# Attention with the keys on the partitions: the exps are used as they come, V is stationary, the mask is added by a matmul

## The chip, the cores and the metric

One core of one Trainium2 chip runs the kernel. The metric is the time of one execution on the device in microseconds (us); the median of the runs stands for the kernel. The engines named below are PE (matmuls and transposes), DVE and ACT (elementwise work; ACT also has the exponential), POOL (constants, selections, and issuing some transfers) and SP, which here only issues transfers. Each works through its own queue in order. Matmul results land in PSUM, eight banks of 512 f32 per partition, and are copied from there to SBUF.

## The reference

Block-sparse attention on 4 batch entries, 8 heads, 768 tokens and a head dimension of 64, and then a mixture of 8 experts of which each token takes one. Everything is f32.

```
scores = q @ k.T / sqrt(64)
mask   = neighbouring 32-blocks, first and last block, 3 sampled blocks per row of blocks
attn   = exp(where(mask, scores, -1e9) - rowmax);  attn /= attn.sum(-1) + 1e-9
x      = (attn @ v), heads side by side            # 3072 tokens x 512
logits = x @ w_gate;  e = argmax;  g = softmax(logits)[e]
out    = g * (relu(x @ w1[e]) @ w2[e])             # w1: 512 x 1024, w2: 1024 x 512
```

The inputs q, k and v are normal numbers times 0.1, so that the scores lie near zero.

## The kernel before, in words

The kernel has three stages. The attention works on 16 pairs of heads (4 batch entries, 4 pairs each). A pair has 6 chunks of 128 tokens; chunk c holds the tokens 6p + c, p being the partition, so that a transfer reads long runs. `load` (L79) fetches k, q and v of a pair through SP, one pair ahead. `turn` (L147) transposes k and q on PE (L155) so that the head dimension lies on the partitions: head 0 on partitions 0 to 63, head 1 on 64 to 127.

A unit is one chunk of 128 queries of a pair; there are 96. `scores` (L165) multiplies the queries as stationary operand with all 768 keys (L173), two matmuls per head. A head has 64 rows of the array, and the two heads' matmuls alternate. One DVE instruction (L181) adds the mask, which lies in SBUF as 0 or -2^33 per query and key, and takes the row's extreme; ACT forms the exps and their sum (L186). Queries are on the partitions at that point, and the next matmul has to contract over keys. So `turn_e` (L190) transposes the 12 blocks of exps on PE (L197) and copies them back in three parts (L199 on DVE, L201 on ACT). `attend` (L205) makes each transposed block stationary and moves the 64 columns of V past it (L209), 12 matmuls per unit, divides by the sums (L213 to L215) and writes 128 columns of x. `route` (L220) transposes the finished x once more (L225, L227) and adds the pair's part of the logits (L230, L235); `keep_x` stores x to DRAM, `gate` the gate weights at a batch entry's end.

The mask is built once at the start: which blocks attend to which (`allow`, with the sampled blocks from DRAM), which query lies in which block (`rows`), their product on PE (L136) and its widening to 768 keys on DVE (L141, L142). The 16 MB of w1 are fetched to SBUF by POOL (L94).

The second stage, the routing (L297 to L411), sorts the tokens by expert: POOL makes constants, DVE computes slots, PE sums (L349, L350, L404). The third stage takes 31 tiles of 128 tokens: POOL gathers their rows of x (L424), SP fetches w2 of the tile's expert (L432), PE runs both layers (L447, L469), POOL scatters the results (L472).

The order of the work is written out in the loop at L268: scores of unit u, transposes of unit u - 1, attend of unit u - 2, route of unit u - 4. A planner then simulates the engines by a cost model and may move an instruction ahead of others on its engine when its operands and buffers come free earlier; it also sets all semaphores. The profile's order on PE thus differs a little from the code's. A buffer that is named with bufs=2 exists twice, and a third use waits until the first is released.

Of the kernel before, what the change touches and what calls it, by code (L numbers as in the profile page):

```python
# [8 lines left out]
F32 = mybir.dt.float32  # L9
# [9 lines left out]
def kernel(  # L19
# [11 lines left out]
    nc = tc.nc  # L31
# [5 lines left out]
    NCH = S // P  # chunks of 128 tokens; chunk c holds the tokens NCH * p + c  # L37
    CW = NCH // 2 * P  # columns of half the chunks, within one PSUM bank
# [31 lines left out]
    ps_t = att.enter_context(tc.tile_pool(name="ps_t", bufs=2, space=PSUM))  # L70
    ps_o = att.enter_context(tc.tile_pool(name="ps_o", bufs=2, space=PSUM))
    ld = att.enter_context(tc.tile_pool(name="ld", bufs=2))
    work = att.enter_context(tc.tile_pool(name="work", bufs=2))
    small = att.enter_context(tc.tile_pool(name="small", bufs=4))
    xpool = att.enter_context(tc.tile_pool(name="xpool", bufs=2))

    loaded, turned = {}, {}

    def load(b, pr):  # L79
        got = []  # L80
        for src, nm in ((k, "k_sb"), (q, "q_sb")):
            t = ld.tile([P, NCH, 2, D], F32, name=nm)
            for hh in range(2):
                nc.sync.dma_start(t[:, :, hh, :], src[b, 2 * pr + hh].rearrange("(p c) d -> p c d", p=P))  # L84
            got.append(t)
        t = ld.tile([P, 2, NCH, D], F32, name="v_sb")
# [6 lines left out]
    def load_w1(e):  # L93
# [4 lines left out]
    mask = mpool.tile([P, NCH, S], BF16, name="mask")  # L98

    def make_mask(pool):  # L100
        # Which blocks of keys (columns) a block of queries (partitions) attends to.
# [24 lines left out]
        # rows[n, t, p]: whether query NCH * p + t lies in block n.  # L126
        rows = pool.tile([NB, NCH, P], F32, name="rows")
        nc.vector.memset(rows[:], 1.0)
        for base, cm, st, sp in ((0, -BLK, 1, NCH), (BLK - 1, BLK, -1, -NCH)):
            nc.gpsimd.affine_select(  # L130
                out=rows[:], in_=rows[:], compare_op=ALU.is_ge, fill=0.0, base=base, channel_multiplier=cm,
                pattern=[[st, NCH], [sp, P]],
            )
        bm = ps_o.tile([P, NCH, NB], F32, name="bm", tag="o")
        for t in range(NCH):
            nc.tensor.matmul(bm[:, t, :], lhsT=rows[:, t, :], rhs=allow[:], start=True, stop=True)  # L136
        pen = pool.tile([P, NCH, NB], F32, name="pen")
        nc.vector.tensor_scalar(pen[:], bm[:], scalar1=-MASKED, scalar2=MASKED, op0=ALU.mult, op1=ALU.add)
        for t in range(NCH):
            wide = pool.tile([P, NB, BLK], BF16, name="wide", bufs=2)  # L140
            nc.vector.tensor_copy(wide[:], pen[:, t, :].unsqueeze(2).to_broadcast([P, NB, BLK]))  # L141
            nc.vector.tensor_copy(  # L142
                mask[:, t, :].rearrange("p (c j) -> p c j", c=NCH),
                wide.rearrange("p n o -> p (n o)").rearrange("p (j c) -> p c j", c=NCH),
            )

    def turn(b, pr):  # L147
        k_sb, q_sb, v_sb = loaded.pop((b, pr))
        outs = []
        for src, nm in ((k_sb, "kT"), (q_sb, "qT")):  # L150
            dst = work.tile([P, S], F32, name=nm)
            for half in range(2):
                tp = ps_t.tile([P, CW], F32, name="tp", tag="t")
                for c in range(NCH // 2):
                    nc.tensor.transpose(  # L155
                        tp[:, c * P : (c + 1) * P], src[:, half * (NCH // 2) + c].rearrange("p h d -> p (h d)"), ident[:],
                    )
                if half == 0:
                    nc.vector.tensor_copy(dst[:, :CW], tp[:])
                else:  # L160
                    nc.scalar.copy(dst[:, CW:], tp[:])
            outs.append(dst)
        turned[(b, pr)] = (*outs, v_sb)

    def scores(b, pr, t):  # L165
        kT, qT, v_sb = turned[(b, pr)]
        ss = small.tile([P, 2], F32, name="ss")
        es = []
        sps = [ps_s.tile([P, 2, 512], F32, name="s") for hh in range(2)]
        for j in range(2):  # L170
            for hh in range(2):
                r = slice(hh * D, (hh + 1) * D)
                nc.tensor.matmul(  # L173
                    sps[hh][:, j, :CW], lhsT=qT[r, t * P : (t + 1) * P], rhs=kT[r, j * CW : (j + 1) * CW],
                    start=True, stop=True,
                )
        for hh in range(2):
            # The scores with their sign turned, and the least of each row: minus its maximum.
            e = work.tile([P, S], F32, name="e", bufs=4)
            nmax = small.tile([P, 1], F32, name="nmax")  # L180
            nc.vector.tensor_tensor_reduce(  # L181
                out=e.rearrange("p (j c) -> p j c", j=2), in0=sps[hh][:, :, :CW],
                in1=mask[:, t, :].rearrange("p (j c) -> p j c", j=2),
                scale=-scale, scalar=3.0e38, op0=ALU.add, op1=ALU.min, accum_out=nmax[:],
            )
            nc.scalar.activation(e[:], e[:], AF.Exp, bias=nmax[:], scale=-1.0, accum_out=ss[:, hh : hh + 1])  # L186
            es.append(e)
        return es, ss, v_sb

    def turn_e(es, ss, v_sb):  # L190
        eT = []
        for g in range(3):
            part = late.tile([P, 4, P], F32, name="eT", bufs=6)
            tp = ps_t.tile([P, 4, P], F32, name="tpe", tag="t")
            for m in range(4):
                hh, c = divmod(4 * g + m, NCH)
                nc.tensor.transpose(tp[:, m, :], es[hh][:, c * P : (c + 1) * P], ident[:])  # L197
            if g == 0:
                nc.vector.tensor_copy(part[:], tp[:])  # L199
            else:  # L200
                nc.scalar.copy(part[:], tp[:])  # L201
            eT += [part[:, m, :] for m in range(4)]
        return eT, ss, v_sb

    def attend(t, eT, ss, v_sb, xb):  # L205
        op = ps_o.tile([P, 2, D], F32, name="op", tag="o")
        for hh in range(2):
            for c in range(NCH):
                nc.tensor.matmul(  # L209
# [316 lines left out]
```

## Time and profile before

| | us |
|---|---|
| runs (3) | 1201.95, 1203.21, 1203.82 |
| median | 1203.21 |
| the profiled execution: span from first to last instruction | 1203.9 |
| of it PE busy, DVE busy, ACT busy, POOL busy | 1131.7, 414.1, 355.5, 73.8 |
| attention, to PE's last matmul of it | about 668 |
| routing, until the experts' first gathered rows land | about 668 to 699 |
| experts | about 699 to 1204 |

The profile has no time of its own beside the span; the span is what the sums below are made against, and it lies 0.7 us above the median of the runs. A matmul on f32 appears in the trace as two weight loads (PEld) and two MATMUL records, one for each pass; a transpose appears as one of each. The duration of a MATMUL record includes the time in the array's pipeline, so that successive records overlap: what a record costs is the distance between starts. "128*64" in a matmul's row is rows times columns of the array that it uses.

### The profile page before, as it was taken

Reading aid. Unit: us, or ns where it says so; the run is one execution under the profiler, and the core shown is the slowest. Engines: PE = TensorE matmul, PEld = TensorE weight load, DVE = VectorE, ACT = ScalarE, POOL = GpSimd, SP = SyncE. Lnnn points to the kernel's source line nnn. Section 1 sums busy time; section 2 is a strip of 40 time slices with the busy share of each in tenths; the row PEclk is TensorE's granted clock in tenths of the full one; section 3 lists DMA queues with packets and bytes.
Section 4 is the critical chain, followed back from the end, with each engine's and each line's share of the span. In section 5 each row is a group of like instructions: output and inputs, shape, how many; then the busy total and the mean of one; then the engine's idle time right before and its main releaser. Section 6 shows DMA issues by size and latency. Waiting matters only on the chain.

```text
span 1203.9 us, 15693 instructions
## 1 busy us (share of the span) xinstructions
PE 1131.7 (94%) x6132; PEld 756.1 (63%) x6132; DVE 414.1 (34%) x1032; ACT 355.5 (30%) x707; POOL 73.8 (6%) x101
## 2 busy tenths in 40 slices
PE   2899999999999999999999579999999999999996
PEld 1687878787877788788878534444444444444443
DVE  1654545554454444454444411111111111111110
ACT  0454545454545455455545000000000000000000
POOL 3000000000000000000000011111110111111100
PEclk9999999999999999999999679999999999999998
DMA  9911221112021212120000415544444555544441
GB/s 337 343 37 27 54 53 28 40 43 53 27 52 30 53 27 54 27 54 27 27 1 14 154 36 174 168 141 160 149 156 164 175 172 175 174 162 149 161 140 55
DMA packets 112269, 122.64 MB, mean 102 GB/s; under 512 B 56451, under 2 KB 72835, under 8 KB 112196
## 3 DMA queue, kind: packets, MB, share of 16 engines
q1 hardware_dynamic: 102484, 90.28, 24.9%
q0 software_dynamic: 9184, 31.33, 6.7%
q8 instruction: 50, 0.82, 0.3%
q14 instruction: 23, 0.19, 0.1%
q10 hardware_dynamic: 528, 0.02, 0.0%
HBM read 108.93 MB, written 14.52 MB: 103 GB/s over the span
## 4 chain that ended last, share of the span: by engine, by line
PE 54%; issue 38%; POOL 3%; DVE 2%; DMA 1%; SPq 0%; POOLq 0%; ACT 0%; DVEq 0%
PE op L209 21%; PE s L173 16%; PE tpe L197 12%; POOL xg L424 3%; PE lg L230 2%; PE tp L155 2%; DMA samp_i<-in_sampled_blocks_dram 1%; POOL out_dram L472 1%; PE tpx L225 1%; PE tok_ps L404 1%; DVE mask L142 0%; DVE wide L141 0%; PE bm L136 0%; SPq L84 0%; DVE oh_r L399 0%
## 5 line engine op out<-in xcount | busy, mean ns | idle before, releaser
L209 PE MATMUL op<-v_sb,eT 128*128 128x64 f32 x2304 | 278.5, 271 | 0.0
L209 PEld LDWEIGHTS op<-v_sb,eT 128*128 128x128 f32 x2304 | 272.4, 192 | 0.0
L186 ACT ACTIVATE e<-e,nmax 128x768 f32<-128x768 f32 x192 | 179.7, 936 | 243.6 <-DVE nmax L181 238.8
L447 PE MATMUL hp<-w_all,xgT 128*128 x496 | 223.2, 604 | 16.4 <-DVE xgT L439 16.4
L469 PE MATMUL zp<-w,hT 128*128 128x512 f32 x496 | 218.2, 593 | 1.1 <-DVE hT L462 1.1
L181 DVE CUSTOM_DVE_ANT_0 e<-s,mask 128x768 f32<-128x768 f32 x192 | 176.3, 954 | 103.2 <-PE s L173 103.2
L173 PE MATMUL s<-kT,qT 64*128 64x384 f32 x768 | 198.3, 525 | 7.8 <-DVE nmax L181 7.8
L447 PEld LDWEIGHTS hp<-w_all,xgT 128*128 128x128 f32 x496 | 92.7, 192 | 129.2 <-issue 105.9
L197 PEld LDWEIGHTS tpe<-ident,e 128*128 128x128 f32 x1152 | 127.5, 145 | 61.1 <-issue 26.7
L197 PE MATMUL tpe<-ident,e 128*128 128x128 f32 x1152 | 164.5, 279 | 0.0
L469 PEld LDWEIGHTS zp<-w,hT 128*128 128x128 f32 x496 | 91.8, 190 | 105.3 <-issue 103.8
L464 ACT COPY hT<-tph 128x512 f32<-128x512 f32 x31 | 18.2, 586 | 436.7 <-PE tph L460 436.7
L201 ACT COPY eT<-tpe 128x512 f32<-128x512 f32 x192 | 110.8, 577 | 51.0 <-PE tpe L197 50.5
L173 PEld LDWEIGHTS s<-kT,qT 64*128 64x128 f32 x768 | 79.2, 188 | 45.1 <-issue 19.6
L471 DVE TENSOR_SCALAR zo<-zp,xg 128x512 f32<-128x512 f32 x31 | 23.3, 750 | 204.3 <-PE zp L469 204.3
L452 DVE TENSOR_SCALAR h<-hp 128x512 f32<-128x512 f32 x31 | 21.4, 691 | 209.0 <-PE hp L447 209.0
L199 DVE COPY eT<-tpe 128x512 f32<-128x512 f32 x96 | 65.9, 687 | 15.5 <-PE tpe L197 15.3
L472 POOL DMA_INDIRECT out_dram<-zo,s_idx x31 | 31.6, 1018 | 431.3 <-DVE zo L471 431.3
L213 DVE TENSOR_SCALAR r<-ss 128x2 f32<-128x2 f32 x96 | 16.1, 167 | 88.1 <-ACT e L186 88.1
L215 DVE TENSOR_TENSOR xb<-op,r 128x128 f32<-128x128 f32 x96 | 28.0, 292 | 43.9 <-PE op L209 42.8
L308 POOL IOTA first_w_i<- 128x8 int32 x1 | 0.1, 135 | 657.4 <-PE op L209 657.4
L460 PEld LDWEIGHTS tph<-ident,h 128*128 128x128 f32 x248 | 30.0, 141 | 16.4 <-issue 16.4
(103 smaller groups left out, 484.0 us busy)
## 6 DMA issues: line engine op xcount, KB each, us to landing
w<-in_moe_w_dram SPq DMA_DIRECT2D x31, 2048.0 KB, 10.4
w_all<-in_moe_w_dram POOLq DMA_DIRECT2D x8, 2048.0 KB, 27.3
k_sb<-in_k_dram SPq DMA_DIRECT2D x32, 192.0 KB, 3.4
q_sb<-in_q_dram SPq DMA_DIRECT2D x32, 192.0 KB, 3.3
v_sb<-in_v_dram SPq DMA_DIRECT2D x16, 384.0 KB, 3.4
x_rows<-xb SPq DMA_DIRECT2D x16, 384.0 KB, 4.3
xg<-x_rows,g_idx POOLq DMA_INDIRECT x31, 7.8
out_dram<-zo,s_idx POOLq DMA_INDIRECT x31, 8.0
```

Source lines behind the costliest of these rows:

```text
L173: nc.tensor.matmul(sps[hh][:, j, :CW], lhsT=qT[r, t * P : (t + 1) * P], rhs=kT[r, j * CW : (j + 1) * CW], start=True, stop=True,)
L181: nc.vector.tensor_tensor_reduce(out=e.rearrange("p (j c) -> p j c", j=2), in0=sps[hh][:, :, :CW], in1=mask[:, t, :].rearrange("p (j c) -> ...
L186: nc.scalar.activation(e[:], e[:], AF.Exp, bias=nmax[:], scale=-1.0, accum_out=ss[:, hh : hh + 1])
L197: nc.tensor.transpose(tp[:, m, :], es[hh][:, c * P : (c + 1) * P], ident[:])
L199: nc.vector.tensor_copy(part[:], tp[:])
L201: nc.scalar.copy(part[:], tp[:])
L209: nc.tensor.matmul(op[:, hh, :], lhsT=eT[hh * NCH + c], rhs=v_sb[:, hh, c, :], start=(c == 0), stop=(c == NCH - 1),)
L424: nc.gpsimd.indirect_dma_start(out=xg[:], out_offset=None, in_=x_d[:, :], in_offset=bass.IndirectOffsetOnAxis(ap=g_idx[:, i : i + 1], axis=0),
L447: nc.tensor.matmul(hp[:, f, :], lhsT=st[i]["xT"][:, c, :], rhs=w1_all[:, c, bass.ds(e, 1), f * 512 : (f + 1) * 512].rearrange("p e f -> p ...
L460: nc.tensor.transpose(tp[:, m, :], st[i]["h"][:, (4 * g + m) * P : (4 * g + m + 1) * P], ident[:])
L469: nc.tensor.matmul(zp[:], lhsT=st[i]["hT"][:, fb, :], rhs=st[i]["w2"][:, fb, :], start=(fb == 0), stop=(fb == FB - 1))
L472: ins = nc.gpsimd.indirect_dma_start(out=out[:, :], out_offset=bass.IndirectOffsetOnAxis(ap=s_idx[:, i : i + 1], axis=0), in_=zo[:], in_of ...
```

## The change

The stationary operand of the scores is now a chunk of 128 keys, the moving one half of the pair's queries (384), so that the scores come out with keys on the partitions and the exps can be contracted over keys without a transpose. The mask is added in PSUM by a second matmul in bf16: `oh` says which block a key lies in, `pen` holds 0 or -2^33 per block and query, twice, on partitions 0 to 63 and 64 to 127. No maximum is subtracted; ACT reads PSUM and takes exp of the scaled scores of both heads at once. DVE adds up the six exps of a half. V (128 keys x 64) is stationary in `attend`; head 0's result goes to partitions 0 to 63 of the output bank and head 1's to 64 to 127, which makes them use the left and the right half of the array's columns. The output is then transposed, and multiplied with the gate's weights, by one matmul per 128 queries with the moving operand `mix` (identity, and w_gate for each head); the sums of the exps are brought onto the query partitions by matmuls with a column of ones. The division is done afterwards, on x and on the logits' parts.

The order is by groups of two chunks of keys: scores of group i, attend of group i - 1; in the middle group of each half also half of the next pair's turn (k in the first half, q in the second) and the output of the half before. Score buffers are two of two banks each, transposes have one bank, outputs of attend two, output turns one. v has three buffers, and the second pair is loaded ahead of the loop.

At the end of the attention a check compares all sums with 2^-4 and 2^40 and all logits with -2^100 and 2^100, counts the entries that pass, and loads the verdict into registers of all engines; under `tc.If` stands a general path that does the attention again with a maximum subtracted. The mask's construction is changed accordingly. Routing and experts are as before. The core of the diff:

```diff
+    ps_t = att.enter_context(tc.tile_pool(name="ps_t", bufs=1, space=PSUM))
+    ps_x = att.enter_context(tc.tile_pool(name="ps_x", bufs=1, space=PSUM))
...
+        nc.vector.tensor_copy(oh[:], rows[:])
+        for half in range(2):
+            bm = ps_o.tile([P, HC, P], F32, name="bm", tag="o")
+            nc.tensor.matmul(bm[:], lhsT=allow2[:], rhs=rows[:NB, half * HC : (half + 1) * HC, :], start=True, stop=True)
+            nc.vector.tensor_scalar(
+                pen[:, half * CW : (half + 1) * CW].rearrange("p (t q) -> p t q", t=HC), bm[:],
+                scalar1=-MASKED, scalar2=MASKED, op0=ALU.mult, op1=ALU.add,
+            )
...
+    def scores(n, half, c):
+        b, pr = pairs[n]
+        kT, qT = turned[(b, pr)][0], turned[(b, pr)][1]
+        cols = slice(half * CW, (half + 1) * CW)
+        s = ps_s.tile([P, 2, 512], F32, name="s")
+        for hh in range(2):
+            r = slice(hh * D, (hh + 1) * D)
+            nc.tensor.matmul(s[:, hh, :CW], lhsT=kT[r, c * P : (c + 1) * P], rhs=qT[r, cols], start=True, stop=False)
+        for hh in range(2):
+            r = slice(hh * D, (hh + 1) * D)
+            nc.tensor.matmul(s[:, hh, :CW], lhsT=oh[r, c, :], rhs=pen[r, cols], start=False, stop=True)
+        e = work.tile([P, 2, CW], F32, name="e", bufs=6)
+        nc.scalar.activation(e[:], s[:, :, :CW], AF.Exp, scale=scale)
+        es[(n, half, c)] = e
+        if c == 1:
+            esums[(n, half)] = work.tile([P, 2, CW], F32, name="esum")
+        if c > 0:
+            t = esums[(n, half)]
+            nc.vector.tensor_add(t[:], es[(n, half, 0)][:] if c == 1 else t[:], e[:])
+
+    def attend(n, half, c):
+        v_sb = loaded[pairs[n]][2]
+        if c == 0:
+            ops_[(n, half)] = ps_o.tile([P, CW], F32, name="op", tag="o")
+        op = ops_[(n, half)]
+        e = es[(n, half, c)]
+        for hh in range(2):
+            nc.tensor.matmul(
+                op[hh * D : (hh + 1) * D, :], lhsT=v_sb[:, hh, c, :], rhs=e[:, hh, :], start=(c == 0), stop=(c == NCH - 1),
+            )
+        if c == NCH - 1:
+            oT = work.tile([P, CW], F32, name="oT")
+            nc.scalar.copy(oT[:], op[:])
+            ops_[(n, half)] = oT
+
+    def rows_out(n, half):
...
+        for m in range(HC):
+            for hh in range(2):
+                nc.tensor.matmul(
+                    xr[:, HC * M + 2 * m + hh : HC * M + 2 * m + hh + 1], lhsT=esum[:, hh, m * P : (m + 1) * P], rhs=ones[:],
+                    start=True, stop=True,
+                )
+        for m in range(HC):
+            nc.tensor.matmul(xr[:, m * M : (m + 1) * M], lhsT=oT[:, m * P : (m + 1) * P], rhs=mix[:, pr, :], start=True, stop=True)
...
+    GR = 2
+    steps = [(n, half, g) for n in range(len(pairs)) for half in range(2) for g in range(NCH // GR)]
+    load(*pairs[1])
+    for i in range(len(steps) + 2):
+        if i < len(steps):
+            n, half, g = steps[i]
+            if half == 1 and g == 0 and n + 2 < len(pairs):
+                load(*pairs[n + 2])
+            if half == 0 and g == 2 and n % 2 == 0 and n // 2 < E:
+                load_w(n // 2)
+            for c in range(g * GR, (g + 1) * GR):
+                scores(n, half, c)
+        if 0 <= i - 1 < len(steps):
+            n, half, g = steps[i - 1]
+            for c in range(g * GR, (g + 1) * GR):
+                attend(n, half, c)
+        if i < len(steps) and steps[i][2] == 1:
+            n, half, _ = steps[i]
+            turning = turn(*pairs[n + 1], half) if n + 1 < len(pairs) else iter(())
+            next(turning, None)
+            if i > 3:
+                rows_out(*steps[i - 2][:2])
+            for _ in turning:
+                pass
+    rows_out(*steps[-1][:2])
...
+    nc.vector.tensor_single_scalar(ok[:, :n_sums], flat, 2.0**-4, op=ALU.is_ge)
+    nc.vector.scalar_tensor_tensor(
+        ok[:, :n_sums], in0=flat, scalar=2.0**40, in1=ok[:, :n_sums], op0=ALU.is_le, op1=ALU.mult,
+    )
...
+    nc.vector.reduce_sum(okn[:], ok[:], axis=AX)
+    okp = ps_x.tile([1, 1], F32, name="okp", tag="xr")
+    nc.tensor.matmul(okp[:], lhsT=okn[:], rhs=ones[:], start=True, stop=True)
+    bad = mpool.tile([1, 1], I32, name="bad")
+    nc.vector.tensor_scalar(bad[:], okp[:], scalar1=float(P * (n_sums + n_lgn)), scalar2=None, op0=ALU.not_equal)
...
+    again = nc.values_load(bad[0:1, 0:1], min_val=0, max_val=1)
+    with tc.If(again > 0):
+        for n in range(len(pairs)):
...
```

## Rows read from the trace of the kernel before

**Rows 1.** The page's first part: busy us, share of the span, instructions of each engine
```profile
PE 1131.7 (94%) x6132; PEld 756.1 (63%) x6132; DVE 414.1 (34%) x1032; ACT 355.5 (30%) x707; POOL 73.8 (6%) x101
```

**Rows 2.** Stretches: us; PE, PEld, DVE, ACT, POOL busy (instructions); granted clock, DMA
```profile
134.00:641.00 507.00, 507.00 (x3763) 408.75 (x3761) 248.90 (x683) 256.80 (x516) 0.00 (x0) 1.00 0.15 38
...
668.00:683.00 15.00, 2.29 (x12) 1.95 (x12) 11.47 (x36) 0.72 (x2) 2.24 (x16) 0.64 0.34 97
```

**Rows 3.** The page's chain that ended last, share of the span by engine
```profile
PE 54%; issue 38%; POOL 3%; DVE 2%; DMA 1%; SPq 0%; POOLq 0%; ACT 0%; DVEq 0%
```

**Rows 4.** Stretch of one pair of heads, between two loads
```profile
254.00:293.60 39.60, 39.60 (x295) 31.87 (x295) 19.16 (x53) 19.89 (x41) 0.00 (x0) 1.00 0.16 41
```

**Rows 5.** Groups by line of that pair: xcount | busy us, mean ns | idle before
```profile
L209 PE MATMUL op<-v_sb,eT 128*128 128x64 f32 x145 | 17.7, 271 | 0.0
...
L173 PE MATMUL s<-kT,qT 64*128 64x384 f32 x48 | 12.3, 517 | 0.0
...
L197 PE MATMUL tpe<-ident,e 128*128 128x128 f32 x72 | 10.2, 278 | 0.0
```

**Rows 6.** Timeline of one unit: start us, us, engine, line, operation, xcount [idle before]
```profile
304.72 1.56 PE L173 MATMUL s<-kT,qT 64*128 64x384 f32 x8
...
306.21 0.86 PEld L197 LDWEIGHTS tpe<-ident,e 128*128 128x128 f32 x8 [0.55 <-issue]
...
307.03 2.09 PEld L209 LDWEIGHTS op<-v_sb,eT 128*128 128x128 f32 x18
```

**Rows 7.** Timeline of PE in ever later windows of the same unit's scores
```profile
305.15 1.14 PE L173 MATMUL s<-kT,qT 64*128 64x384 f32 x6
...
305.47 0.81 PE L173 MATMUL s<-kT,qT 64*128 64x384 f32 x4
...
305.79 0.49 PE L173 MATMUL s<-kT,qT 64*128 64x384 f32 x2
```

**Rows 8.** Groups by line over the whole span
```profile
L186 ACT ACTIVATE e<-e,nmax 128x768 f32<-128x768 f32 x192 | 179.7, 936 | 243.6 <-DVE nmax L181 238.8 <-DVE gw L254 4.8
...
L227 ACT COPY xT<-tpx 128x384 f32<-128x384 f32 x32 | 15.3, 479 | 15.1 <-PE tpx L225 15.1
...
L399 DVE TENSOR_TENSOR oh_r<-iota_r,rc 128x768 f32<-128x768 f32 x4 | 3.6, 953 | 0.0
```

**Rows 9.** Lines L94 and, in the window at 21.5 us, L84: issues and landings
```profile
L94 POOL DMA_DIRECT2D w_all<-in_moe_w_dram x8: 740/750/941, 2.8 to 9.7; - x8
...
DMA to landing us min/median/max: 11.8/27.3/45.7
...
L84 SPq DMA_DIRECT2D q_sb<-in_q_dram x1: 8193/8193/8193, 21.5 to 21.5; - x1
...
DMA to landing us min/median/max: 31.8/31.8/31.8
```

**Rows 10.** Timeline at the attention's end
```profile
667.84 0.29 DVE L215 TENSOR_TENSOR xb<-op,r 128x128 f32<-128x128 f32 x1 [2.55 <-PE op L209]
...
670.68 0.36 DVE L334 TENSOR_TENSOR sc<-lgn,lmax 128x192 f32<-128x192 f32 x1
...
676.81 0.16 DVE L370 CAST xe<-xe_f 1x31 int32<-1x31 f32 x1
...
678.27 1.65 SPq L432 DMA_DIRECT2D w<-in_moe_w_dram  x2
```

**Rows 11.** The page's transfers: xcount, KB each, us to landing
```profile
x_rows<-xb SPq DMA_DIRECT2D x16, 384.0 KB, 4.3
...
wg<-in_moe_w_gate_dram ACTq DMA_DIRECT2D x1, 16.0 KB, 1.9
```

**Rows 12.** Stretch 683 to 693 us; timeline of L447's first weight loads
```profile
683.00:693.00 10.00, 10.00 (x48) 10.00 (x48) 0.94 (x2) 0.00 (x0) 0.00 (x0) 0.50 0.85 317
...
702.16 0.34 PEld L447 LDWEIGHTS hp<-w_all,xgT 128*128 128x128 f32 x1 [0.52 <-issue]
703.01 0.34 PEld L447 LDWEIGHTS hp<-w_all,xgT 128*128 128x128 f32 x1 [0.52 <-issue]
```

More of the change, by code (lines that the diff above doesn't have):

```diff
@@ L85, in load @@
             got.append(t)
-        t = ld.tile([P, 2, NCH, D], F32, name="v_sb")
+        t = ld.tile([P, 2, NCH, D], F32, name="v_sb", bufs=3)
         nc.sync.dma_start(
@@ L137, in make_mask @@
[L137 to L170, printed above, removed]
+        allow2 = pool.tile([NB, P], F32, name="allow2")
+        nc.vector.memset(allow2[:], 0.0)
+        nc.vector.tensor_copy(allow2[:, :NB], allow[:])
+        nc.vector.tensor_copy(allow2[:, D : D + NB], allow[:])
+        rows = pool.tile([P, NCH, P], F32, name="rows")
@@ new lines, with turn @@
+    small = att.enter_context(tc.tile_pool(name="small", bufs=4))
+    xpool = att.enter_context(tc.tile_pool(name="xpool", bufs=2))
+    def turn(b, pr, which):
+        src = loaded[(b, pr)][which]
+        dst = work.tile([P, S], F32, name="qT" if which else "kT")
+        turned.setdefault((b, pr), {})[which] = dst
+        for half in range(2):
+            tp = ps_t.tile([P, CW], F32, name="tp", tag="t")
+            for c in range(HC):
+                nc.tensor.transpose(
+                    tp[:, c * P : (c + 1) * P], src[:, half * HC + c].rearrange("p h d -> p (h d)"), ident[:],
+                )
+            if half == 0:
+                nc.vector.tensor_copy(dst[:, :CW], tp[:])
+            else:
+                nc.scalar.copy(dst[:, CW:], tp[:])
+            yield
@@ L188, in scores @@
[L188 to L209, printed above, removed]
-                    op[:, hh, :], lhsT=eT[hh * NCH + c], rhs=v_sb[:, hh, c, :], start=(c == 0), stop=(c == NCH - 1),
-                )
-        r = small.tile([P, 2], F32, name="r")
-        nc.vector.tensor_scalar_add(r[:], ss[:], 1e-9)
-        nc.vector.reciprocal(r[:], r[:])
+        for m in range(HC):
+            nc.tensor.matmul(xr[:, m * M : (m + 1) * M], lhsT=oT[:, m * P : (m + 1) * P], rhs=mix[:, pr, :], start=True, stop=True)
@@ L215, in attend @@
+        lg = small.tile([P, HC, 2, E], F32, name="lg")
         nc.vector.tensor_tensor(
[L216 to L231 removed]
+            lg[:], got[:, :, P:].rearrange("p m (h e) -> p m h e", h=2), r[:].unsqueeze(3).to_broadcast([P, HC, 2, E]), op=ALU.mult,
+        )
@@ L241, in gate @@
+        if half == 1:
+            rows = x_d[b * S : (b + 1) * S, pr * P : (pr + 1) * P]
+            nc.sync.dma_start(rows.rearrange("(p c) w -> p c w", p=P), xb[:])
+            if pr == NPR - 1:
+                gate(b)
     def gate(b):
@@ new lines @@
+    for which in range(2):
+        for _ in turn(0, 0, which):
+            pass
[22 more added lines that the diff above has]
+            for _ in turning:
+                pass
@@ L295 @@
+    again = nc.values_load(bad[0:1, 0:1], min_val=0, max_val=1)
+    with tc.If(again > 0):
+        for n in range(len(pairs)):
+            load(*pairs[n])
+            for which in range(2):
+                for _ in turn(*pairs[n], which):
+                    pass
+            for half in range(2):
+                shifted(n, half)
+                for c in range(NCH):
+                    attend(n, half, c)
+                rows_out(n, half)
     att.close()
```

159 lines of the change are left out of this document (83 added, 76 removed).

## The prediction

> **What bounds the kernel now.** I read the page's busy times first, then the stretches, then the chain, then one pair of heads record by record. PE is busy 94% of the span, DVE 34%, ACT 30% [rows 1]. The stretches divide the span: from 134 to 641 us, inside the attention, PE is busy for every microsecond at a granted clock of 1.00; the routing behind it has PE at work for 2.3 of 15 us and a clock that falls [rows 2]. The change touches the attention and the seam behind it, so the attention's PE time is what counts. The chain agrees: PE has 54% of it, and no other engine over 3% [rows 3]; its 38% "issue" is the time before matmuls of the experts for which nothing is waited, and these stay as they are.
>
> One pair of heads takes 39.6 us, PE without a gap, DVE and ACT at half load [rows 4]. By line it is the 144 records of L209 (one matmul on f32 shows as two records, one per pass), the 48 of L173, the 72 transposes of L197 and small change [rows 5].
>
> How PE spends a record is seen in one unit [rows 6, 7]. The scores use 64 rows of the array per head, and the two heads start together: of eight records from 304.72 six are left at 305.15, four at 305.47, two at 305.79. The spacing is 0.322 us, so one f32 pass of 384 columns costs 0.839 ns a column, and two heads cost what one does. The 18 L209 weight loads of 2.09 us come every 0.112 us or so, though a record moves only 64 columns (0.054 us by the same 0.839 ns): attend is bound by loading its weights. The transposes keep much the same pace (8 from 306.21 to 307.03); I count 0.11.
>
> **The change, part by part.** I call 128 keys by 384 queries of both heads a step: 12 per pair, 192 in all.
> Removed per pair: the 72 transposes of exps (72 x 0.11 = 7.9 us of PE), their copies on DVE and ACT, 144 attend records (144 x 0.112 = 16.1 us), the mask and maximum on DVE, six route transposes.
> Scores of a step: the same kind of matmul, keys and queries exchanged: two passes of 0.322 us, heads side by side, 0.645 us.
> Mask of a step: two bf16 matmuls of 384 columns on 64 rows each, side by side as the scores are. The trace has no bf16 matmul. Above, one pass at the f32 pace, 0.32 us; below, one weight load, 0.11 us. I take 0.20, near the middle, as one short pass of narrow operands. The Trainium skill, "TensorE: Matmul & The Clock Gate", section "Back-to-back issue gap", gives columns / 2.4 + 2.5 ns for a warm bf16 matmul, an estimate of 162 ns here, by which the forecast would be 981 us; no run here shows it yet.
> Attend of a step: V stationary, 64 columns, one half of the array's columns per head, 384 columns moving in two passes. If the halves run side by side as the row halves do, 0.645 us; one after the other, 1.29 us. I take 0.645: the row halves are the nearest thing the trace shows [rows 7]. The Trainium skill, "TensorE: Matmul & The Clock Gate", section "Measured speedup vs the span model", has three column tiles at 2.38 times the pace of one, 79% of the full gain; an estimate by it is 0.81 us a step and 1018 us in all. No row of this trace has a column tile.
> Change of array shape: steps come in groups of two, scores then attend, so two changes a group. The eight score records hold PE for 1.49 us where four spacings are 1.29, 0.20 too much; the weight loads behind them idle 0.55 us [rows 6]. Between 0.20 and 0.55 I take 0.35 a group.
> A group is 2 x (0.645 + 0.20 + 0.645) + 0.35 = 3.33 us; three make 9.99 us for half a pair's queries.
> Added per half, the output's turn: six sums (12 records with a one-column operand, bound by weight loads as L209's, 12 x 0.112 = 1.34 us) and three matmuls of 144 columns (6 x 0.121 = 0.73 us): 2.06 us. Six transposes of the next pair's k or q: 0.65 us, and 0.2 us for the shape. Half: 12.9 us; pair: 25.8 us.
>
> What hides the rest. ACT per half: six exps of 768 columns, 0.94 us each as now, and two copies of 384 columns, 0.48 us each: 6.6 us. DVE per half: five adds of 768 columns at 0.953 us (L399 is that size), a copy of 384, and eight small operations, at most 0.3 us each, behind the turn: 7.7 us at most [rows 8]. Both lie under 12.9 us. Two score buffers of two banks suffice: a buffer is free one exp, some 1.1 us, after its mask, and PE comes back to it after one attend group, 1.3 us, and another step. The single transpose buffer makes the second three transposes wait for DVE; the output's turn stands between. If that cover went, it would cost PE a DVE add and a copy, some 1.5 us a half, 45 us in 30 halves.
>
> The start. Eight loads of w1 leave POOL by 9.7 us and the last lands 45.7 us later, at 55.4; behind them the second load of the second pair's q, issued at 21.5, lands after 31.8 us, at 53.3 [rows 9]. It is issued so early already that moving the second pair's loads ahead of the loop brings nothing, and w1 goes through POOL's queue as before. So even if pair 0 were started by 25 us and took 25.8, it would be done before pair 1 can begin, and part of its gain is lost. Pair 1 starts after six transposes of q and two copies (0.7 and 2 x 0.5 us) with a wait or two between, at 55.5.
> PE is through at 55.5 + 15 x 25.8 = 442.5 us.
>
> The seam. Today 2.8 us pass from the last xb to the router's first operation at 670.7 [rows 10]. The check adds five DVE operations (about 2.0 us at the 0.36 us of L334's 192 columns), a matmul and a compare (1.2, an estimate from four steps of about 0.3) and a load of the verdict into every engine's registers (1.3: xe is done at 676.97, the transfer that needs it issues at 678.27 [rows 10]): 4.5 us, with the 2.8 7.3 us. Then every engine branches over the general path. POOL's constants, 2.2 us that lay beside the attention's end [rows 2], start behind it; the router needs them one after the other, so they cost little. Nothing in the trace shows such a branch; below zero is excluded, since it only adds a wait. I allow a landing of a row write (4.3 us) and of a short load (1.9 us) [rows 11]: 6.2; the top is 16. Routing starts at 442.5 + 13.5 = 456.0.
> From there to the end 1203.9 - 670.7 = 533.2 us are unchanged: routing runs at clock 0.50 already [rows 12], so a longer idle stretch ahead takes nothing more. 456.0 + 533.2 = 989.2. The profiled execution spans 1203.9, the median of the runs is 1203.2: 988.5 us.
>
> **The rivals.**
> Columns one after the other. V's halves may not overlap: they read two different streams over all 128 partitions, where the row halves read 64 each [rows 7]. Against it: the halves of the array are as separate. Price 0.645 us x 180 steps = 116 us: 1104 us.
> The clock falls: slower than before. While the 48 small matmuls of L404 kept PE busy for 10 of 10 us, the clock stayed at 0.50, the lower of its levels of 1.2 and 2.4 GHz, and passes of 512 columns then started 0.85 us apart where 0.839 ns a column gives 0.43 [rows 12]. If half-filled arrays did that throughout, a pair would take 51.6 us: 55.5 + 774 + 13.5 + 533.2 = 1376 us. It outweighs the gain of 215 us once more than 8 of the 15 pairs run so (215 / 25.8). Against it: the row-halved scores run at 1.00 from 134 to 641 us [rows 2].
> The change doesn't do what it says: the verdict is wrong and the general path runs as well. Per half at least six blocks of 1.29 + 0.4 + 0.65 us, attend 3.9 and the turns 2.7, 21 us; 32 of them, 660 us: 1650 us or more. Against it: the sums count some hundred exps near one, far inside their limits, and the counts stay whole numbers.
>
> **How the numbers follow.** Forecast, columns side by side: 0.74, own range 950 to 1040. Its low end: mask 0.11 (-16), shape change 0.20 (-14), branch free (-6). Its high end: mask 0.32 (+22), change 0.55 (+18), branch 16 (+10). Columns in turn 0.18, around 1104. A cover gone or a finer alternation by the planner, 1040 to 1075: 0.04. Clock 0.03, general path 0.01. The range 950 to 1110 takes in the second case. Faster by over 0.2% (about what a measurement can tell from no change) 0.955, slower 0.04, the same 0.005.
>
> **What would show it.** Right: attend's records (128 rows by 64 columns) start in twos, the twos 0.32 us apart; pairs follow every 25 to 27 us with PE busy throughout at clock 1.00; DVE and ACT near half; routing begins near 456 us; the last 533 us as before. Wrong: attend records one by one 0.32 us apart (pairs of 33.5 us); a clock of 0.50 in the attention; mask records near 0.32 us; PE idle before scores with ACT or DVE as releaser, which would mean that the cover failed; a seam over 25 us.

## The result and the profile after

The changed kernel takes 969.39 us (median of 4 runs, 968.87 to 969.55) where the kernel before takes 1202.58 (1200.7 to 1203.82) beside it: a ratio of 0.8057, 95% interval 0.8046 to 0.8069. The forecast was 988.5, its range 950 to 1110. The profiled execution spans 967.7 us, which stands to the 989.2 of the prediction's sum.

The page's busy times of the changed kernel; the line answers to [rows 1].

```profile
PE 901.3 (93%) x4110; PEld 458.7 (47%) x4110; DVE 321.4 (33%) x621; ACT 221.5 (23%) x323; POOL 76.4 (8%) x103
```

A third of PE's records are gone (6132 to 4110) and more than half of ACT's (707 to 323); PE's busy time falls by 230.4 us, and the span by 236.2. No other engine has come near its limit.

Stretches of the changed kernel: us; PE, PEld, DVE, ACT and POOL busy (instructions); granted clock, DMA share, GB/s. They answer to [rows 2, 4].

```profile
60.00:400.00 340.00, 340.00 (x2260) 181.60 (x2260) 182.70 (x363) 156.37 (x218) 0.00 (x0) 1.00 0.25 61
200.00:225.30 25.30, 25.30 (x171) 13.49 (x171) 13.43 (x26) 11.64 (x16) 0.00 (x0) 1.00 0.26 63
426.00:435.00 9.00, 0.19 (x2) 0.11 (x2) 3.69 (x20) 0.24 (x1) 0.07 (x1) 0.58 0.22 54
```

PE is busy in every microsecond from 60 to 400 us, inside the attention, and at clock 1.00, as before. The second line is one pair of heads, the length that the turn's records repeat at: 25.30 us where [rows 4] have 39.6, with DVE at 13.4 and ACT at 11.6. The third is the seam: 9 us in which PE works for 0.19.

One group of two steps in the changed kernel's timeline (start us, us, engine, line, operation, xcount [idle before]); it answers to [rows 6].

```profile
208.47 0.92 PE L195 MATMUL s<-qT,kT 64*128 64x384 f32 x4
209.22 0.33 PE L198 MATMUL s<-pen,oh 64*128 64x384 bf16 x2
209.39 0.81 PE L195 MATMUL s<-qT,kT 64*128 64x384 f32 x4
209.59 1.68 ACT L200 ACTIVATE e<-s 128x768 f32<-128x768 f32 x2 [1.64 <-PE s L198]
210.03 0.33 PE L198 MATMUL s<-pen,oh 64*128 64x384 bf16 x2
210.29 1.51 PE L215 MATMUL op<-e,v_sb 128*64 128x384 f32 x8
211.73 0.59 PE L195 MATMUL s<-qT,kT 64*128 64x384 f32 x2
```

Read the starts. The second step's scores take from 209.39 to 210.03, 0.64 us; a mask from 209.22 to 209.39, 0.17; the eight attend records from 210.29 to 211.73, 1.44 us. The group takes 211.73 - 208.47 = 3.26 us. Three of them with the turn make a half of 12.65.

The same eight attend records in ever later windows, read as [rows 7] were.

```profile
210.66 1.14 PE L215 MATMUL op<-e,v_sb 128*64 128x384 f32 x6
210.99 0.81 PE L215 MATMUL op<-e,v_sb 128*64 128x384 f32 x4
211.31 0.49 PE L215 MATMUL op<-e,v_sb 128*64 128x384 f32 x2
```

Eight are left at 210.29, six at 210.66, four at 210.99, two at 211.31: they start in twos, 0.32 us apart. The two column halves run side by side.

### The profile page after: what moved, and what is told of

Read it like the earlier page. It is cut to its first block, busy times and chain, and to the rows that moved or that the text cites. A ratio compares the mean times of both kernels' runs of the same rounds, so it can differ in the third digit from the quotient of the medians.

```text
span 967.7 us, 10826 instructions
## 1 busy us (share of the span) xinstructions
PE 901.3 (93%) x4110; PEld 458.7 (47%) x4110; DVE 321.4 (33%) x621; ACT 221.5 (23%) x323; POOL 76.4 (8%) x103
## 4 chain that ended last, share of the span: by engine, by line
issue 47%; POOL 5%; PE 1%; DVE 1%; POOLq 0%; DVEq 0%
POOL xg L512 3%; POOL out_dram L560 1%; PE tok_ps L492 1%; DVE oh_r L487 0%; POOLq L609 0%; DVE oh_c L479 0%; DVE oh_c L483 0%; POOLq L512 0%; DVE sl L467 0%; POOLq L560 0%; DVE pr__10054 L432 0%; PE cps L437 0%; PE cps L438 0%; POOL lt_strict L409 0%; DVE xk L452 0%
## 5 line engine op out<-in xcount | busy, mean ns | idle before, releaser
L200 ACT ACTIVATE e<-s 128x768 f32<-128x768 f32 x192 | 155.3, 811 | 94.8 <-PE s L198 93.1
L195 PE MATMUL s<-qT,kT 64*128 64x384 f32 x768 | 167.4, 514 | 0.0
L206 DVE TENSOR_TENSOR esum<-esum,e 128x768 f32<-128x768 f32 x128 | 122.6, 958 | 71.5 <-ACT e L200 64.5
L215 PE MATMUL op<-e,v_sb 128*64 128x384 f32 x768 | 144.8, 499 | 0.0
L195 PEld LDWEIGHTS s<-qT,kT 64*128 64x128 f32 x768 | 64.1, 188 | 64.8 <-ACT e L200 38.0
L215 PEld LDWEIGHTS op<-e,v_sb 128*64 128x64 f32 x768 | 46.6, 136 | 80.1 <-issue 79.9
L198 PE MATMUL s<-pen,oh 64*128 64x384 bf16 x384 | 63.8, 326 | 0.0
L231 PEld LDWEIGHTS xr<-ones,esum 128*128 128x128 f32 x384 | 45.4, 192 | 1.8 <-DVE esum L206 1.2
L231 PE MATMUL xr<-ones,esum 128*128 128x1 f32 x384 | 45.0, 244 | 0.0
L548 PE MATMUL tph<-ident,h 128*128 128x128 f32 x248 | 36.9, 273 | 0.0
```

The source lines that it names most:

```text
L195: nc.tensor.matmul(s[:, hh, :CW], lhsT=kT[r, c * P : (c + 1) * P], rhs=qT[r, cols], start=True, stop=False)
L198: nc.tensor.matmul(s[:, hh, :CW], lhsT=oh[r, c, :], rhs=pen[r, cols], start=False, stop=True)
L200: nc.scalar.activation(e[:], s[:, :, :CW], AF.Exp, scale=scale)
L206: nc.vector.tensor_add(t[:], es[(n, half, 0)][:] if c == 1 else t[:], e[:])
L215: nc.tensor.matmul(op[hh * D : (hh + 1) * D, :], lhsT=v_sb[:, hh, c, :], rhs=e[:, hh, :], start=(c == 0), stop=(c == NCH - 1),)
L231: nc.tensor.matmul(xr[:, HC * M + 2 * m + hh : HC * M + 2 * m + hh + 1], lhsT=esum[:, hh, m * P : (m + 1) * P], rhs=ones[:], start=True, s ...
```

## The experiments

Theory: PE sets the pace throughout the attention. Steps cost 1.45 us of PE (0.645, 0.16 and 0.645), two changes of array shape 0.36 a group, the turn 2.9 a half; the heads run side by side in rows (scores) and in columns (attend); DVE and ACT are covered; the start gained by the order of loads, the seam lost to the check. Rivals: the column halves are worth nothing and something else is faster than thought; ACT or the two score buffers pace the groups; the start's gain comes from the attention's new form. Ratios are to the kernel before beside each run.

**Both heads in one column half** (the results are summed, so attend's output is another; the copy behind it is changed to match: ACT copies 64 partitions out of PSUM, and DVE copies them to the other 64).

```diff
-                op[hh * D : (hh + 1) * D, :], lhsT=v_sb[:, hh, c, :], rhs=e[:, hh, :], start=(c == 0), stop=(c == NCH - 1),
+                op[:D, :], lhsT=v_sb[:, hh, c, :], rhs=e[:, hh, :], start=(c == 0 and hh == 0), stop=(c == NCH - 1 and hh == 1),
```

> Both heads' attend matmuls go to the left half of the array's columns and are summed in one output (so x is not the reference's: the heads are mixed); all else as in the changed kernel at 969.4 us. Theory (the column halves run side by side, and PE sets the pace): the pairs of records come apart, each step's attend takes 4 x 0.322 = 1.29 us instead of 0.645, so 192 x 0.645 = +124 us, about 1093 us, and a pair of heads takes 33.0 us instead of 25.3. Rival (the starts in twos are how the records are drawn, the array works on the halves in turn anyway): no change, 969 us. Second rival (ACT's exps set the pace): under +60 us.

Measured 1093.56 us, ratio 0.9093 [0.9076, 0.9109]. Its timeline, the whole run of records and its last two windows:

```profile
205.49 2.79 PE L215 MATMUL op<-e,v_sb 128*64 128x384 f32 x8
207.47 0.81 PE L215 MATMUL op<-e,v_sb 128*64 128x384 f32 x2
207.80 0.49 PE L215 MATMUL op<-e,v_sb 128*64 128x384 f32 x1
208.21 0.55 PE L176 MATMUL tp<-ident,q_sb 128*128 128x128 f32 x3
```

Now they start one by one, 0.33 us apart, and eight take 208.21 - 205.49 = 2.72 us in place of 1.44. The 124 us are 192 steps of 0.645: what the prediction called columns side by side is shown, and without it over half of the 233 us of gain would be gone.

**No mask matmuls** (the mask is left out of the scores).

```diff
-            nc.tensor.matmul(s[:, hh, :CW], lhsT=kT[r, c * P : (c + 1) * P], rhs=qT[r, cols], start=True, stop=False)
-        for hh in range(2):
-            r = slice(hh * D, (hh + 1) * D)
-            nc.tensor.matmul(s[:, hh, :CW], lhsT=oh[r, c, :], rhs=pen[r, cols], start=False, stop=True)
+            nc.tensor.matmul(s[:, hh, :CW], lhsT=kT[r, c * P : (c + 1) * P], rhs=qT[r, cols], start=True, stop=True)
```

> The mask's bf16 matmuls are left out, so every query attends to every key (the output is not the reference's). Theory (PE sets the pace, a mask pair costs 0.162 us on it): 192 x 0.162 = -31 us, about 938 us, and a pair of heads takes 23.4 us. Rival (the exps on ACT, or the chain from scores over exps to attend, set the pace): no gain, 967 to 970 us.

Measured 940.09 us, ratio 0.7826 [0.781, 0.7843]: 29.3 us less, 0.153 for each of 192 steps. A record taken from PE shortens the time by its own length, so PE paces, not ACT or DVE.

**Groups of one chunk.**

```diff
-    GR = 2
+    GR = 1
```

> GR = 1: scores and attend alternate after every chunk of keys instead of every second one, twice as many changes between row halves and column halves. Theory (two changes cost 0.36 us, whatever stands between them): 96 more pairs of changes, +34 us, about 1003 us. Rival (the 0.36 us is a wait for buffers or exps that comes once per group of any size): with groups of one, the scores wait for an exp sooner, so more than +34 us, with idle time of PE put down to ACT. Second rival (the weight loads behind a change are hidden): 969 us.

Measured 1032.37 us, ratio 0.8589 [0.8573, 0.8604], 29 us over the expectation. PE's timeline, first around a turn's end, then a steady step:

```profile
200.38 0.91 PE L195 MATMUL s<-qT,kT 64*128 64x384 f32 x2
201.22 0.55 PE L176 MATMUL tp<-ident,k_sb 128*128 128x128 f32 x3
201.69 0.59 PE L195 MATMUL s<-qT,kT 64*128 64x384 f32 x1
...
202.12 0.48 PE L195 MATMUL s<-qT,kT 64*128 64x384 f32 x1
...
202.70 0.87 PE L215 MATMUL op<-e,v_sb 128*64 128x384 f32 x4
203.49 0.92 PE L195 MATMUL s<-qT,kT 64*128 64x384 f32 x4
...
204.50 0.87 PE L215 MATMUL op<-e,v_sb 128*64 128x384 f32 x4
205.29 0.92 PE L195 MATMUL s<-qT,kT 64*128 64x384 f32 x4
```

A steady step takes 205.29 - 203.49 = 1.80 us, 1.452 + 0.35: the changes of shape cost what was said, 34 us. The rest is not a wait for ACT. The planner has put three transposes between the two heads' scores, so that the heads run one after the other: from 200.38 to 202.70 are 2.32 us, less 0.47 for the transposes 1.85, where a whole pair takes 204.50 - 203.49 = 1.01. That is 0.84 a half, 27 us in 32 halves, read from the trace; the same size of group with the order held was not run.

**Every exp twice.**

```diff
-        nc.scalar.activation(e[:], s[:, :, :CW], AF.Exp, scale=scale)
+        for again in range(2):
+            nc.scalar.activation(e[:], s[:, :, :CW], AF.Exp, scale=scale)
```

> Each exp is done twice by ACT, the same operands and output. Theory (ACT has 5.8 of 12.65 us per half a pair and two score buffers suffice): ACT comes to 10.7 us per half, still under PE's 12.65; the buffer of a group's second scores is then free only about when PE wants it, 0 to 0.2 us late in each of 96 groups: 969 to 990 us. Rival (ACT's exps stand on the path): 192 x 0.81 = +156 us, 1125 us.

Measured 1010.48 us, ratio 0.8403 [0.8388, 0.8418], above the theory's upper end and far under the rival. A stretch, and PE's timeline from one half's turn on:

```profile
60.00:400.00 340.00, 339.29 (x2052) 171.61 (x2048) 166.13 (x327) 251.15 (x347) 0.00 (x0) 1.00 0.24 60
```

```profile
209.02 0.91 PE L195 MATMUL s<-qT,kT 64*128 64x384 f32 x2
209.86 0.55 PE L176 MATMUL tp<-ident,q_sb 128*128 128x128 f32 x3
...
212.14 1.51 PE L216 MATMUL op<-e,v_sb 128*64 128x384 f32 x8
213.58 0.92 PE L195 MATMUL s<-qT,kT 64*128 64x384 f32 x4
214.33 0.33 PE L198 MATMUL s<-pen,oh 64*128 64x384 bf16 x2
214.69 0.92 PE L195 MATMUL s<-qT,kT 64*128 64x384 f32 x4
...
215.70 0.54 PE L216 MATMUL op<-e,v_sb 128*64 128x384 f32 x2
```

ACT is now busy for 251 of 340 us, and PE for all but 0.7. The half takes 1.28 us more than 12.65 (turn to turn, 209.02 to 222.95), 41 us in 32. Two places are seen: transposes between the two heads' scores again (scores to attend take 3.12 us where 1.82 and 0.47 for the transposes would do: +0.83), and the next group's second scores 0.20 late at 214.69 with a restart of 0.1 (2.12 in place of 1.82: +0.30); 0.15 of the 1.28 is not placed. So, as read from the trace, twice the exps delay the groups by about 0.3 us a half, and the greater part goes with the planner's new order; this run doesn't part the two cleanly.

**Groups of three chunks** (with the middle group's work in the second group).

```diff
-    GR = 2
+    GR = 3
...
-            if i > 3:
+            if i > 1:
                 rows_out(*steps[i - 2][:2])
```

> The changed kernel with groups of three chunks of keys in place of two (two groups a half; the turn and the output of the half before stand in the second). Theory: the pace of a group is records plus 0.355 us for its two shape changes, unless the score buffers run out. A third step needs the first step's buffer: after the group's first score record at 0, the first mask is at 0.75, its exp starts at 1.12 and ends at 1.93 (208.47, 209.22, 209.59, 210.40 in the changed kernel's trace), and PE would come to the third scores at 0.92 + 0.81 = 1.73: a wait of 0.2 to 0.3 us a group. A half of two groups is then 2 x (4.356 + 0.355 + 0.25) = 9.92 us where three groups of two take 9.78: +0.14 x 32 = +4 us, 974 us, with PE's idle before the third scores put to ACT. Rival: two buffers do for any group, the exps keep up; then one change pair of 0.355 us a half is saved, 32 x 0.355 = 11 us: 958 us, PE without a gap. Second rival, from the groups of one: the planner takes the turn apart and the time rises by over 20 us, with transposes between single scores.

Measured 981.27 us, ratio 0.8147 [0.8127, 0.8166]. PE's timeline of one group:

```profile
199.75 0.92 PE L195 MATMUL s<-qT,kT 64*128 64x384 f32 x4
...
201.31 0.33 PE L198 MATMUL s<-pen,oh 64*128 64x384 bf16 x2
201.73 0.92 PE L195 MATMUL s<-qT,kT 64*128 64x384 f32 x4
202.48 0.33 PE L198 MATMUL s<-pen,oh 64*128 64x384 bf16 x2
202.74 2.16 PE L215 MATMUL op<-e,v_sb 128*64 128x384 f32 x12
204.82 0.92 PE L195 MATMUL s<-qT,kT 64*128 64x384 f32 x4
```

```profile
200.87 1.68 ACT L200 ACTIVATE e<-s 128x768 f32<-128x768 f32 x2 [0.53 <-PE s L198]
```

The third scores start at 201.73 where the second mask's 0.162 end at 201.47: a wait of 0.26, as the theory had it. In the second extract, ACT's, the first exp starts at 200.87 and, at 0.81 us, ends at 201.68, just ahead of the third scores, which need its buffer. The profile books little of this as idle time of PE, since the mask's records still run. What the theory missed is that scores after a wait take 0.75 to their mask and not 0.65. A group is 5.07 us (4.96 expected), a half 13.03, and 0.38 over 12.65 in 32 halves is 12 us: the whole difference. Two buffers suffice for groups of two and not for three; what a pair of changes saves is lost to the buffer. The planner kept the turn whole, so the second rival is out.

**w1 early in the changed kernel** (its loads behind the identity, ahead of the mask's selections).

```diff
+    for e in range(E):
+        nc.vector.tensor_copy(w1_all[:, 0, e, 0:1], ident[:, 0:1])
+        load_w(e)
...
-            if half == 0 and g == 2 and n % 2 == 0 and n // 2 < E:
-                load_w(n // 2)
```

> The changed kernel with w1's eight loads leaving POOL behind the identity, at about 3 us as in the kernel before, ahead of three of the four selections that stand before them in the changed kernel (6.9 us). Theory (the start gained 11.5 us over the forecast only because the first pairs' loads and the block list overtook w1): the block list lands near 19 us instead of 8, the second pair's q near 53 instead of 24, the second pair starts near 55 instead of 44 us: +11 us, about 980 us. Rival (the start is set by building the mask and by PE's lower clock there): 968 to 971 us.

Measured 979.93 us, ratio 0.8154 [0.8139, 0.8169]: the size is right. The way is not, by the timelines of DVE and PE:

```profile
8.57 0.16 DVE L125 CAST samp<-samp_i 24x3 f32<-24x3 int32 x1 [3.28 <-DMA samp_i<-in_sampled_blocks_dram]
...
25.64 1.65 PE L198 MATMUL s<-qT,kT 64*128 64x384 f32 x4
...
46.14 0.52 PE L179 MATMUL tp<-ident,q_sb 128*128 128x128 f32 x3 [2.02 <-DMA q_sb<-in_q_dram]
```

The first load leaves at 4.79 us and not near 3, behind that of the block list (4.66), so the list is cast at 8.57 and not near 19. The eight issues hold POOL from 4.79 to 10.95 us, the selections come late, and the first scores start at 25.64 in place of 19.68; later PE waits 2.0 us for pair 1's q, and the granted clock is 0.80 to 0.85 from 44 to 54 us. Pair 1's first scores come at 53.88 in place of 43.98: of the 9.9 us 6.0 are POOL's late selections, and the other 3.9 are the wait for q and the slower work behind it. So this run doesn't put back the state of the kernel before; that the size fits is in part chance.

**The kernel before with w1 late** (its loads wait for the block list, and are issued there instead of in the loop).

```diff
+        for e in range(E):
+            nc.vector.tensor_copy(w1_all[:NB, 0, e, 0:1], samp[:, 0:1])
+            load_w1_all(e)
```

> The kernel before, with w1's loads made to wait for the block list (a small DVE copy from it into each of them). Theory (10 to 12 us of the start hang on the order of the loads, not on the form of the attention): the list lands near 8 us instead of 19, the mask is ready near 20 instead of 31 us, and the kernel takes 1191 to 1194 us. Rival (what the start gains is lost to waits for the second pair's k and q, as w1 then competes with them): 1200 to 1204 us.

Measured 1192.75 us, ratio 0.9913 [0.99, 0.9927], 10 us less than the 1202.94 beside it; the list is cast at 8.39 us in place of 19.36. The order of loads is worth some 10 us in the kernel before, which could have had them without the change.

**The check and the general path left out.**

```diff
-    again = nc.values_load(bad[0:1, 0:1], min_val=0, max_val=1)
-    with tc.If(again > 0):
...
```

> The check, the load of its verdict and the general path are left out (on these inputs the output stays the reference's). Theory (the seam's 8.9 us from PE's last matmul to the router's first operation are a 4.0 us branch on PE and a wait for the last row write, behind a check of some 3 us): the seam is 2.9 us as before the change, -6 us, about 963 us. Rival (the routing's constants on POOL and the row writes hold the router up anyway): 967 to 969 us.

Measured 960.48 us, ratio 0.7986 [0.7975, 0.7997]. Its stretches around the attention's end:

```profile
400.00:425.00 25.00, 25.00 (x167) 13.67 (x162) 12.50 (x24) 9.66 (x14) 0.00 (x0) 1.00 0.06 17
425.00:427.10 2.10, 0.04 (x1) 0.00 (x0) 1.82 (x9) 0.00 (x0) 1.51 (x11) 0.63 0.00 0
```

The router's first operation starts at 427.12, 2.1 us behind PE's last matmul, and POOL makes its constants meanwhile. Check, branch and general path cost 8.9 us, 6.9 of them in the seam; the other 2.0 lie ahead of it and behind it, about 1.0 each, without a cause shown (PE's last matmul ends at 425.0 here, at 426.0 in the changed kernel and at 424.7 in the next run, whose attention is the same). With the whole mask in place this is the fastest version measured; it has no general path.

**A general path of one pair in place of 16** (it does not run here).

```diff
-        for n in range(len(pairs)):
+        for n in range(1):
             load(*pairs[n])
```

> The changed kernel whose general path redoes one pair of heads instead of all 16 (it does not run here: the branch over it is taken). PE's branch took 4.0 us in the changed kernel, those of the other engines 0.05 to 0.07. Theory: PE's branch is long because of the block of PE's instructions that it passes over; with a sixteenth of it the branch record falls below 1 us. The time hardly changes all the same, 968.5 to 969.5 us, since SP's first semaphore behind the branch waits for the last row write (issued 429.93, landed 434.1), which ends together with PE's branch; the router's first operation comes 0 to 0.8 us earlier. Rival: the 4.0 us do not depend on the block (a branch on PE costs that much, or waits for something else); the record stays at about 4 us and the time at 969.4 us. Second rival: the write is not what the router waits for, and it starts over 2 us earlier: 966 to 967 us.

Measured 967.73 us, ratio 0.8069 [0.8018, 0.8121]; the four runs lie between 966.86 and 981.11, so the time can't tell the three forecasts of 966 to 969.5 apart. PE's branch record, beside the changed kernel's further down:

```profile
L372 PEldq COMPARE_BRANCH  x1: 3924/3924/3924, 429.1 to 429.1; - x1
```

My theory falls: with a sixteenth of the path PE's branch still takes 3.92 us. The rival stands: between these two sizes the block makes no difference. What it waits for is open. In the branch's own window the trace shows transfers of the instruction queues (0.03 MB here, 0.06 MB in the changed kernel), which fits a fetch of the code behind the branch, but no run took that fetch away. What the router waits for is not parted either: the row write is issued at 429.79 here and lands 3.2 us later, the branch ends at 433.0 too, and the router starts at 433.21.

**Sums by a stationary of ones** (64 columns of ones per head, sums on all partitions of a head, division ahead of the turn, the turn's transposes split over two groups): an attempt at a faster version.

```diff
+            nc.tensor.matmul(sp[hh * D : (hh + 1) * D, :], lhsT=ones[:], rhs=esum[:, hh, :], start=True, stop=True)
+        r = work.tile([P, CW], F32, name="r")
+        nc.vector.reciprocal(r[:], sp[:])
...
+        nc.vector.tensor_tensor(oT[:], op[:], r[:], op=ALU.mult)
```

> The changed kernel, with the sums brought over the keys by a stationary tile of 64 columns of ones (one matmul of 384 columns per head, the heads in the two column halves, right behind attend) in place of six matmuls that make the sums' tile stationary; x is divided by them before it is turned, so the turn moves 136 columns in place of 144; the check looks at the least and greatest reciprocal. The next pair's transposes are split over two groups. Theory (six tiles of 128 stationary columns cost 1.34 us a half, two halves side by side 0.645): per half 3 x 3.26 + 0.65 + 0.68 + 0.66 + two changes of about 0.2 = 12.2 us instead of 12.65, -14 us, about 955 us. Rival (the reciprocal of 384 columns and the division, now on DVE between attend and the turn, are late for PE): 969 us or more, with PE waiting for oT.

Measured 986.73 us (982.63 to 992.65), ratio 0.819 [0.8161, 0.8219]: 17 us more, where 14 less were expected. Its groups by line from 60 to 400 us:

```profile
L224 DVE RECIPROCAL r<-sp 128x384 f32<-128x384 f32 x26 | 66.5, 2557 | 5.8 <-PE sp L222 5.8
...
L237 PE MATMUL xr<-mix,oT 128*128 128x136 f32 x162 | 25.2, 292 | 21.0 <-DVE oT L228 21.0
```

The reciprocal of 384 columns takes 2.56 us, so the divided output is late and PE idles 21 us in that stretch, 0.8 a half or some 26 us in 32. The rival had it; the idle time brings the expected 955 to 981, and the rest is open.

## Why the prediction was right, and where its terms were off

**The pair of heads.** Right. Scores of a step 0.645 forecast, 0.64 measured; attend 0.645, shown by the twin starts and by the 124 us that go when one half is used; change of shape 0.35, measured 3.26 - 2 x 1.452 = 0.36; output's turn, transposes and its change 2.91, measured 12.65 - 3 x 3.26 = 2.87. The mask was set at 0.20, between 0.11 and 0.32, and is 0.15 to 0.17: a bf16 pass of 384 columns takes half of an f32 pass of the same width. The pair is 25.30 us against 25.8 forecast and 39.6 before [rows 4]; 14.3 x 16 = 229 us of the 236 come from there. The estimate of 162 ns for a mask pass, from the Trainium skill, "TensorE: Matmul & The Clock Gate", section "Back-to-back issue gap", whose formula there is for an isolated matmul, is met by the run without masks (0.153 a step) and by the starts 209.22 and 209.39. The estimate of 0.81 us for attend, from the Trainium skill, the same page, section "Measured speedup vs the span model", is not met: the section has three tiles of 32 columns, and the two of 64 here lose nothing, their twin starts being 0.32 us apart as the row halves' are.

**The cover.** Right. ACT's exps are 0.811 us from PSUM (0.94 was taken [rows 8]), DVE's adds 0.958; both engines are half busy, and exps done twice delay the groups by about 0.3 us a half (the rest of that run's 41 us goes with the planner's order). The limit is nearer on the buffers: a third step in a group already waits 0.26 us.

**The start.** This is the term that was furthest off, and the reading behind it was wrong. The prediction has pair 1's first scores at 55.5 us, behind a q that lands at 53.3, since "w1 goes through POOL's queue as before". It does not: the changed mask has four selections of rows where there were two, and w1's first load, which in [rows 9] leaves POOL at 2.8 us, comes behind all four. POOL's timeline in the changed kernel, and DVE's cast of the block list:

```profile
5.22 0.89 POOL L141 TENSOR_SCALAR_AFFINE_SELECT rows<-rows 64x768 f32<-64x768 f32 x1
...
6.88 0.95 POOL L93 DMA_DIRECT2D w_all<-in_moe_w_dram  x1
```

```profile
8.31 0.47 DVE L122 CAST samp<-samp_i 24x3 f32<-24x3 int32 x1 [1.46 <-DMA samp_i<-in_sampled_blocks_dram]
```

By 6.88 all loads that pair 0, the mask and pair 1's scores need are issued but one of q (7.2), ahead of w1's 16 MB: the block list is cast at 8.31 us (19.36 before), the first scores start at 19.68, and pair 1's at 43.98. Pair 1's q, issued by 7.2, lands by 24.2; PE doesn't wait for it, and pair 1 starts when pair 0's work is through. The term was mis-sized by 43.98 - 55.5 = -11.5 us. The kernel before with w1 late shows that there the order of loads is worth 10 us. The run with w1 early comes to 10.5 us, but over half of that by POOL's late selections, so the loads' own share in the changed kernel is not shown by it.

**PE's end.** 426.0 against 442.5: -11.5 from the start, 15 x 0.5 = -7.5 from the pairs, and +2.5 that the sum left out: after the last pair's scores the last group's attend and the last half's output still follow, which elsewhere stand in the next half.

**The seam.** 13.5 us forecast, 434.95 - 426.0 = 8.95 measured. The forecast added the check's 4.5 to the 2.8 of the last half's own work. The timeline shows them side by side: the check's first operation (L321) stands ahead of the last xb (L246), and so on in turn.

```profile
426.33 0.22 DVE L321 TENSOR_SCALAR ok<-sums 128x192 f32<-128x192 f32 x1
426.47 0.61 DVE L246 TENSOR_TENSOR xb<-xr,r 128x192 f32<-128x192 f32 x2
...
434.95 0.36 DVE L422 TENSOR_TENSOR sc<-lgn,lmax 128x192 f32<-128x192 f32 x1 [5.04 <-SPq L372]
```

The verdict is ready at 429.8 and the branches start at 430.3, 4.3 us behind PE's last matmul where 7.3 were allowed. The branches, by line, engine, operation, xcount and ns:

```profile
L372 ACTq COMPARE_BRANCH  x1: 50/50/50, 430.3 to 430.3; - x1
L372 POOLq COMPARE_BRANCH  x1: 45/45/45, 430.4 to 430.4; - x1
L372 PEldq COMPARE_BRANCH  x1: 4004/4004/4004, 430.4 to 430.4; - x1
L372 DVEq COMPARE_BRANCH  x1: 72/72/72, 430.4 to 430.4; - x1
```

The branch costs under 0.1 us on three engines and 4.0 us on PE, and a row write that SP waits for ends with it (issued at 429.93, 4.2 us to landing). From the branches to the router are 4.65 us, where I had allowed 6.2 for the landing of a row write and of a short load, one behind the other. So 3.0 us of the error are the overlap and 1.55 the allowance. POOL's constants, forced behind the branch, cost the router two short waits (0.32 and 0.52 us before DVE's second operation and its scan), so "they cost little" holds.

**The rest.** 967.7 - 434.95 = 532.75 against 533.2. The idle seam takes nothing from routing or experts, as [rows 12] let expect.

The errors add up: -11.5 - 5.0 - 4.6 - 0.4 = -21.5, from 989.2 to 967.7. But for the 2.5 us that the sum left out they point the same way, so the forecast is not near by errors that cancel: the mask and the branch had been put near the middle of their bounds, the start was read off the old kernel's loads, and the seam was added where it overlaps.

## What to carry to other kernels

When PE paces, choose which operand stays so that what must be contracted next comes out on the partitions: it spares the transposes and their copies; put two heads in row halves when the contraction is 64 deep, and in column halves when the output is 64 wide, and check in the trace that the records start in twos. Group work of one array shape, but no further than the buffers between it and the next engine allow, and look at the planner's order: three transposes between two heads' matmuls undid the pairing there. When an edit lengthens work on a queue that also issues bulk loads, count whom these loads now let pass.

## What the runs showed of the hardware that was not expected

A taken branch cost 0.045 to 0.072 us on ACT, POOL and DVE and 3.9 to 4.0 us on PE, whether it passed over 16 pairs' code or one's; why is open. The Trainium skill, "Advanced Engine Details and Errata", section "Control Flow Timing", gives some 108 ns for a compare-and-branch; the three engines lie below that, PE far above.

DVE's reciprocal took 2557 ns for 384 columns of f32 from PSUM, where a multiplication of the same width took 547: it belongs where columns are few, as in the changed kernel's six per half.
